# A state-space convolution beside a gated feed-forward on one core: plain loads turned by PE, paired exponentials, phases by constants, and a new order

## The chip, the cores and the metric

One core of a Trainium2 chip runs the kernel. The metric is the device time of one execution in microseconds (us), lower is better. The engines are PE (matmuls), PEld (its weight loads), DVE (VectorE), ACT (ScalarE), POOL (GpSimd) and SP, which issues most DMAs.

## The reference

Two branches get the same input u (2048 x 640, bf16) and are mixed by a gate per row.

```python
g = sigmoid((u * gate_w).sum(-1))
# branch A: a long convolution per channel d (640), kernel K from 128 complex modes n
dt = exp(log_dt);  logdA = dt * (A_re + 1j*A_im)
K[d, l] = real(sum_n C[d,n] * exp(logdA[d,n] * l) * dt * B[d,n])      # l = 0..2047
a = causal_conv(u, K) + u * Dskip                                     # by FFT of 4096
# branch B: gated feed-forward, F = 1728
b = (gelu(u @ w_gate) * (u @ w_up)) @ w_down
out = g * a + (1 - g) * b
```

## The kernel before, in words

The channels are cut into five parts of 128. The modes n lie on the partitions while the table for K is made. l is split as l = a + b: 21 coarse values a (A_OF, line 23) and 32 fine values, multiples of 8 (b_of, line 33). For each group of parts (0 and 1, 2 and 3, 4 alone: GROUPS, line 313) the kernel makes

- the magnitudes exp(a x value) on ACT (exps, line 289; 32 fine values in eB, 21 coarse ones in eA, one instruction each, over 256 elements a partition for two parts and 128 for one). a32 is A_re x dt, b32 is A_im x dt in parts of a turn (scaled_a, line 283);
- the phases on DVE as integers (trig, line 322): for coarse values one scalar_tensor_tensor a value (L337), for the 17 fine values one broadcast product a chunk with a column of values xv (L340), a quarter turn added (L344), then two sines on ACT (L352), whose low 16 bits wrap by themselves;
- the products of the two (ktable, line 447: L462 to L479), which PE then contracts over n (contract, line 483) to K, written to DRAM and gathered back (gather, line 502).

The convolution is done with matrices of sines and cosines (dft_matrix, line 387, ten in DFT and one that becomes ME) as matmuls: u folded and transformed (u_fold, u_forward), K transformed (k_forward), spectra multiplied on DVE (products, line 665), transformed back (inverse) and unfolded to the output with the feed-forward's part and Dskip's added by PE (unfold, line 724). The feed-forward's first half is ffn_up (line 511): 56 units of ten matmuls of 512 columns, from u transposed (xT) and weights, each copied out of PSUM by ACT or DVE and stored to DRAM (GUd); its second half is glu_load, glu (gelu on ACT, product on DVE) and down.

Everything is ordered by the list ORDER (line 37), whose steps a loop at the end walks. A step is a letter, one or two numbers and, where there is a copy out of PSUM, the engine for it: A for ACT, D for DVE, M for half and half. s starts the sine reciprocal, a is scaled_a, e exponentials, v the products of B and C (phase_and_size), r0 to r2 square root, half angle and angle, t trig, q ktable, c contract, w gather, u ffn_up, m a matrix, F U K P I J Z the convolution's stages, l G D the feed-forward's second half, h the gate, L the load of w_down, and ! releases memory for the next stage. The helpers table() and first() hold the order of ACT's table functions and of DVE's first steps; for the rest, the trace shows that an engine's order is not always the list's (L340 of a later step runs in the middle of v).

The beginning stands ahead of the list, in lines 205 to 308. SP loads log_dt, then A, C, B (re and im) with six transposing DMAs (loadT, line 195) and u with ten more (load_x, line 200), so that xT is in place by DMA alone. POOL issues the first weights and small vectors and zeroes a part of GUd (line 234). DVE fills small columns (c2, ncol, msk, lines 250 to 278) and makes flip, flipn and diag, from POOL's iotas.

Of the kernel before, what the change touches and what calls it, by code (L numbers as in the profile page):

```python
# [9 lines left out]
ALU = mybir.AluOpType  # L10
ACT = mybir.ActivationFunctionType
FP32 = mybir.dt.float32
# [25 lines left out]
s a e03 v e00 e13 e01 uA e04 r0 uD e02 e10 e15 uD uD uD r1 t05 uD uD uD r2 uD uD e12 uD uD e14 uD uD uA !0 uA e11 uA  # L38
uA uA e05 uA t04 q04 t06 t01 t02 q06 uD t07 uA q07 uA uA uA uA q05 t00 q00 uA m uA uA uA q02 t03 q01 t14 q03 c00A !1 m
uD c02A c01A uA t16 c10A w0 c11D uA c12A t10 uA uA m uA uA uA uA t15 uA t17 uD uD m q10 q15 uD uA m uD t11 e21 uA uD  # L40
e25 e23 e20 e24 uD q14 e22 t12 uA q16 uA q12 t13 m q17 w1 uA m uA q13 uA q11 uD c20A c21A m c22A m c30A c32A uA m t22
c31A uA w3 m !2 t20 F0P U00A q20 t21 U02A U03A t23 K00D l00 K01A U01A G00 h q22 w2 q21 q23 L c40A !3 c41A F1A U10A
D00A c42A U12A l01 U11A K10A U13A F2A U20A P00 K11A l10 G01 P01 U23A K20A D01A P10 U22A F3A D03D P02 I00A w4 P03 G10
D02A P11 U21A U30A P12 U31A K21A J10A U32D U33D D10A D11A l11 G11 P20 F4A P13 l20 D13D I01A J11A D12A G20 Z00A Z01M
K30A U40A K40A I11A l21 P21 U42A D20A K31A P22 P23 D21A l30 J20A J21A G21 K41A D23D G30 D22A P30 l31 P31 Z02A U43A
U41A D30A P32 D31A P40 P33 J22A G31 I30D P41 J23A D32A D33A J33A P42 Z11A Z03A J32A J40A J41A P43 Z12A Z10A Z20D J43D
Z13M J42A Z21M Z23A Z22D
# [4 lines left out]
def kernel(  # L52
# [49 lines left out]
    last_first = [None]  # L102

    def first(inst):
# [6 lines left out]
        return inst  # L111

# [23 lines left out]
    NMAT = 10  # L136
    DFT = cp.tile([128, NMAT, 2, 512], BF16, name="DFT")
    ME = cp.tile([128, 3, 2, 512], BF16, name="ME")
    diag = cp.tile([128, KT_, 128], BF16, name="diag")
# [5 lines left out]
    nc.vector.memset(KTt[:, 5], 0.0)  # L145
# [30 lines left out]
    NT = 3  # L176
    wg_v = B_w_gate.rearrange("(k p) f -> p k f", p=128)
# [22 lines left out]
    def load_x(hf):  # L200
        for kt in range(KT_):
            nc.sync.dma_start_transpose(out=xT[:, kt, 1024 * hf:1024 * (hf + 1)],  # L202
                                        in_=u2[1024 * hf:1024 * (hf + 1), kt * 128:(kt + 1) * 128])

    fr_i = pw.tile([128, 2, 2, 128], I32, name="fr_i")
# [6 lines left out]
    first(nc.vector.tensor_copy(out=tcol[:], in_=tcol_i[:]))  # L212
    fr = pd.tile([128, 512], FP32, name="fr")
    first(nc.vector.tensor_scalar(out=fr[:], in0=fr_i[:].rearrange("p a b q -> p (a b q)"), scalar1=TURN / 4096.0,
                                  scalar2=None, op0=ALU.mult))

    ldt = pw.tile([N, D], BF16, name="ldt")
# [8 lines left out]
    load_x(0)  # L226
    load_x(1)
    dskc = pw.tile([128, KT_], BF16, name="dskc")
    nc.gpsimd.dma_start(out=dskc[:], in_=A_Dskip.rearrange("(k p) -> p k", p=128))
    nc.gpsimd.dma_start(out=gwc[:], in_=gate_w.rearrange("(k p) -> p k", p=128))  # L230
    zero = pw.tile([128, 2, 512], BF16, name="zero")
    nc.gpsimd.memset(zero[:], 0.0)
    for c in range(4):
        nc.gpsimd.dma_start(out=GUd[c][FR:128, NFULL], in_=zero[FR:128])
# [4 lines left out]
    nc.vector.tensor_copy(out=xv[:], in_=xv_i[:])  # L239

# [5 lines left out]
    par_i = pw.tile([128, 1], I32, name="par_i")  # L246
    nc.gpsimd.iota(par_i[:], pattern=[[0, 1]], base=0, channel_multiplier=1)
    hi_i = pw.tile([128, 1], I32, name="hi_i")
    b_i = pw.tile([128, 1], I32, name="b_i")
    nc.vector.tensor_scalar(out=hi_i[:], in0=par_i[:], scalar1=16, scalar2=None, op0=ALU.bitwise_and)  # L250
    nc.vector.tensor_scalar(out=hi_i[:], in0=hi_i[:], scalar1=0, scalar2=15, op0=ALU.is_gt, op1=ALU.mult)
    nc.vector.tensor_scalar(out=b_i[:], in0=par_i[:], scalar1=31, scalar2=None, op0=ALU.bitwise_and)
    tt(out=b_i[:], in0=b_i[:], in1=hi_i[:], op=ALU.bitwise_xor)
    nc.vector.tensor_scalar(out=par_i[:], in0=b_i[:], scalar1=1, scalar2=None, op0=ALU.bitwise_and)
    b16 = pw.tile([128, 1], FP32, name="b16")
    nc.vector.tensor_scalar(out=b16[:], in0=b_i[:], scalar1=16.0, scalar2=None, op0=ALU.mult)
    ncol = pd.tile([128, 5], FP32, name="ncol")
    c2 = pd.tile([128, 7], FP32, name="c2")
    nc.vector.tensor_scalar(out=c2[:, 0:5], in0=c2_i[:], scalar1=b16[:], scalar2=None, op0=ALU.add)
    nc.vector.tensor_copy(out=c2[:, 5:6], in_=c2[:, 4:5])  # L260
    for q, vals in ((0, (3, 1, 3, 1)), (1, (5, 3, 5, 3))):
        for g in range(4):
            nc.vector.memset(ncol[32 * g:32 * g + 32, q:q + 1], float(vals[g]))
    nc.vector.tensor_scalar(out=ncol[:, 2:3], in0=par_i[:], scalar1=-2.0, scalar2=9.0, op0=ALU.mult, op1=ALU.add)
    nc.vector.tensor_copy(out=ncol[0:64, 3:4], in_=ncol[0:64, 2:3])
    nc.vector.memset(ncol[64:128, 3:4], 0.0)
    nc.vector.memset(ncol[:, 4:5], 0.0)
    nc.vector.memset(c2[:, 6:7], 0.0)
    msk = pd.tile([128, 3], FP32, name="msk")
    nc.vector.memset(msk[:], 0.0)  # L270
    for x in range(3):
        nc.vector.memset(msk[32 * x:32 * x + 1, x:x + 1], 1.0)

    for mq, nq, r, c2v, nv in ((2, 0, 0, 256 + 257, 2), (3, 1, 0, 512 + 514, 3), (4, 2, 32, 1024 + 1028, 5),
                               (5, 3, 32, 1022 + 1028, 7), (5, 3, 64, 1532 + 1535, 4),
                               (6, 4, 0, 2 * 511, 1), (6, 4, 32, 1022 + 1023, 2), (6, 4, 64, 2044 + 2047, 4)):
        nc.vector.memset(c2[r:r + 1, mq:mq + 1], float(c2v))
        nc.vector.memset(ncol[r:r + 1, nq:nq + 1], float(nv))
    dtb = pw.tile([N, D], BF16, name="dtb")
    a32 = pp.tile([N, D], FP32, name="a32")  # L280
    b32 = pp.tile([N, D], FP32, name="b32")

    def scaled_a():
        table(nc.scalar.activation(out=dtb[:], in_=ldt[:], func=ACT.Exp))
        first(tt(out=a32[:], in0=AreT[:], in1=dtb[:], op=ALU.mult))  # L285
        first(nc.vector.scalar_tensor_tensor(out=b32[:], in0=AimT[:], scalar=TURN / (2.0 * math.pi), in1=dtb[:],
                                             op0=ALU.mult, op1=ALU.mult))

    def exps(p0, np_, x0, x1):

        src = a32[:, p0 * DP:(p0 + np_) * DP]
        dA, dB = tabs[p0 // 2]
        for x in range(x0, min(x1, NB_ + NA)):
            if x < NB_:
                table(nc.scalar.activation(out=dB[:, 0:np_, :, x, :],  # L295
                                           in_=src.rearrange("n (p g d) -> n p g d", p=np_, d=4),
                                           func=ACT.Exp, scale=float(8 * b_of(x))))
            else:
                table(nc.scalar.activation(out=dA[:, 0:np_, x - NB_, :], in_=src.rearrange("n (p d) -> n p d", p=np_),
                                           func=ACT.Exp, scale=float(A_OF[x - NB_])))  # L300

    make_identity(nc, ident[:])
    fl_i = pw.tile([128, 128], I32, name="fl_i")
    nc.gpsimd.iota(fl_i[:], pattern=[[1, 128]], base=-127, channel_multiplier=1)
    nc.vector.tensor_scalar(out=flip[:], in0=fl_i[:], scalar1=0.0, scalar2=None, op0=ALU.is_equal)
    nc.vector.tensor_scalar(out=flipn[:], in0=flip[:], scalar1=-1.0, scalar2=None, op0=ALU.mult)
    tt(out=diag[:], in0=ident[:, None, :].to_broadcast([128, KT_, 128]),
       in1=dskc[:, :, None].to_broadcast([128, KT_, 128]), op=ALU.mult)

    CW = 12  # L310
    CH2 = ((0, 6), (6, 11), (11, 16), (16, NA), (NA, NA + 5), (NA + 5, NA + 9), (NA + 9, NA + 13), (NA + 13, NA + NK))
    CH1 = ((0, 11), (11, NA), (NA, NA + 9), (NA + 9, NA + NK))
# [9 lines left out]
    def trig(g, ci):  # L322
# [12 lines left out]
        if x1 <= NA:  # L335
            for x in range(n):
                nc.vector.scalar_tensor_tensor(out=ph[:, x, :], in0=b32[:, dsl], scalar=float(A_OF[x0 + x] + MID),  # L337
                                               in1=phi[:, dsl], op0=ALU.mult, op1=ALU.add)
        else:
# [105 lines left out]
    past = []  # L445

    def ktable(g, ci):
        if g not in kqt:
            n = len(GROUPS[g])
            kqt[g] = (pools["kq"].tile([N, n, NA, DP], BF16, name="Q"), pools["kq"].tile([N, n, GP, NB_, 4], BF16, name="sB"))  # L450
        Q, sB = kqt[g]
# [18 lines left out]
        kn = min(k1, 16)  # L470
# [253 lines left out]
    def unfold(z, c, eng):  # L724
# [11 lines left out]
        for h, perm in enumerate(((ident, ident), (flip, flipn))):  # L736
# [4 lines left out]
            for i, k in enumerate(ko):  # L741
                for x, part in enumerate(ZG[z]):
                    nc.tensor.matmul(pZ[:, h, W * i + DP * x:W * i + DP * (x + 1)], lhsT=xt_tile(part, c, k),
                                     rhs=diag[:, part, :], start=False, stop=False)
# [10 lines left out]
    def turn_over(x):  # L755

        if x == 0:
            ictx.__exit__(None, None, None)
# [5 lines left out]
        elif x == 2:  # L764
# [6 lines left out]
            pools.update(ub=es, pm=es, spec=es)  # L771
            pools["Wd"] = wp.tile([128, NFT, D], BF16, name="Wd")
# [17 lines left out]
    for step in ORDER.split():  # L790
# [4 lines left out]
        past.append(step)  # L795
        if kind in "qt":
# [93 lines left out]
```

## Time and profile before

| what | us |
|---|---|
| median of 3 runs (338.11 to 339.29) | 338.71 |
| the profiled execution, its own time | 336.79 |
| its span | 335.0 |
| busy: PE, DVE, ACT, POOL | 288.1, 307.9, 259.5, 11.1 |
| first full run of PE's matmuls | from 22.24 |
| a32 made on DVE (L285) | at 10.16 |
| first product of spectra (L676) | at 188.2 |
| last join of them (L685) | ends 321.8 |

A row of a group reads: line, engine, operation, output<-input with shapes, count | busy us, mean ns of one | idle time before, and what ended it. A row of a timeline begins with start and duration. In a chain of waits each row is a piece of the chain that ended last: start, length, what. Busy shares in 40 slices are in tenths.

### The profile page before, as it was taken

The numbers are of one execution on the slowest core, as the hardware profiler recorded it, in microseconds if no ns is written. First come the engines' busy times: TensorE is split into PE (matmuls) and PEld (weight loads), VectorE is DVE, ScalarE is ACT, GpSimd is POOL, SyncE is SP. The second block draws the span as 40 slices with busy tenths as digits, with TensorE's granted clock in tenths as the row PEclk, the third lists the DMA queues.
The fourth block names the chain that finished last, engine by engine and source line by source line (L and its number), as shares of the span: only waits on it lengthen the run. The fifth ranks groups of instructions, "written<-read, shape, count | busy, mean of one in ns | idle before, by whom it ended". The sixth has DMA issues, their size and how long they took to land.

```text
span 335.0 us, 6177 instructions
## 1 busy us (share of the span) xinstructions
PE 288.1 (86%) x2380; PEld 176.6 (53%) x2380; DVE 307.9 (92%) x443; ACT 259.5 (77%) x414; POOL 11.1 (3%) x41
## 2 busy tenths in 40 slices
PE   0059799999999999997377996999999999999994
PEld 0014344444465444445226755685766778677773
DVE  7685999999999999989999998899999997999962
ACT  4668999997998999998799657867576575852653
POOL 8400000000000000000000000000000000000000
PEclk9999999999999999999559997999999999999999
DMA  8998565646637876624699467555446433260133
GB/s 118 217 194 212 165 203 175 225 150 203 188 125 187 197 222 203 180 100 102 121 306 259 114 170 135 150 154 156 125 115 165 119 112 112 80 173 2 49 93 80
DMA packets 106588, 51.54 MB, mean 154 GB/s; under 512 B 50400, under 2 KB 99616, under 8 KB 106560
## 3 DMA queue, kind: packets, MB, share of 16 engines
q1 hardware_dynamic: 106112, 49.98, 56.7%
q0 software_dynamic: 448, 1.18, 1.8%
q8 instruction: 18, 0.29, 0.4%
q14 instruction: 10, 0.08, 0.1%
HBM read 29.39 MB, written 18.16 MB: 142 GB/s over the span
## 4 chain that ended last, share of the span: by engine, by line
DVE 40%; PE 35%; ACT 8%; issue 6%; SPq 5%; DMA 5%; DVEq 0%; ACTq 0%
PE gu L660 11%; PE gu L522 9%; DVE ph L337 4%; DVE GU L121 4%; PE cv L718 3%; DVE Tp L676 3%; SPq L197 3%; DVE Mb L681 3%; PE cv L603 2%; DVE eB L479 2%; PE cv L585 2%; DVE ph L344 2%; PE cv L739 2%; SPq L202 2%; ACT GU L117 2%
## 5 line engine op out<-in xcount | busy, mean ns | idle before, releaser
L522 PE MATMUL gu<-xT,Wg 128*128 128x512 bf16 x280 | 72.5, 387 | 24.8 <-DMA xT<-in_A_u_dram 19.9
L660 PE MATMUL gu<-Wd,HT 128*128 128x320 bf16 x448 | 66.4, 299 | 0.0
L522 PE MATMUL gu<-xT,Wu 128*128 128x512 bf16 x260 | 66.1, 385 | 0.0
L522 PEld LDWEIGHTS <-Wg 128*128 128x128 bf16 x280 | 27.3, 98 | 59.3 <-issue 21.4
L660 PEld LDWEIGHTS <-HT 128*128 128x128 bf16 x448 | 43.3, 98 | 18.4
L352 ACT ACTIVATE T<-ph 128x1280 bf16<-128x1280 int16 (+4 forms) x40 | 48.0, 1223 | 3.5 <-DVE ph L337 2.6
L522 PEld LDWEIGHTS <-Wu 128*128 128x128 bf16 x260 | 25.7, 99 | 33.3 <-issue 3.9
L117 ACT CAST GU<-gu 128x1024 bf16<-128x1024 f32 (+1 forms) x34 | 32.8, 969 | 6.0 <-PE gu L522 6.0
L676 DVE TENSOR_TENSOR Tp<-Uf,Kf 128x6144 bf16<-128x6144 bf16 (+2 forms) x15 | 34.3, 2288 | 0.0
L647 ACT ACTIVATE HT<-HT 128x1792 bf16<-128x1792 bf16 x16 | 26.7, 1696 | 9.7 <-DMA HT<-GUd 9.6
L121 DVE CAST GU<-gu 128x1024 bf16<-128x1024 f32 (+1 forms) x22 | 26.4, 1200 | 4.9 <-PE gu L522 4.8
L295 ACT ACTIVATE eB<-a 128x256 bf16<-128x256 f32 (+1 forms) x96 | 27.1, 373 | 4.2 <-DVE a L285 4.2
L603 PE MATMUL cv<-KTt,DFT 128*128 128x128 bf16 x280 | 24.9, 221 | 5.7 <-ACT Kf L119 2.8
L681 DVE TENSOR_TENSOR Mb<-Mb,Tp 128x4096 bf16<-128x4096 bf16 (+1 forms) x15 | 29.0, 1935 | 0.3
L119 ACT ACTIVATE ob<-gu,rat 128x640 bf16<-128x640 f32 x13 | 10.2, 793 | 21.8 <-PE gu L660 19.6
L585 PE MATMUL cv<-pm,DFT 128*128 128x512 bf16 x80 | 22.4, 407 | 3.3 <-ACT pm L566 1.5
L603 PEld LDWEIGHTS <-DFT 128*128 128x128 bf16 x280 | 21.3, 99 | 3.1 <-issue 1.9
L119 ACT ACTIVATE Kf<-cv 128x512 bf16<-128x512 f32 x34 | 18.0, 598 | 2.9 <-PE cv L603 2.9
L337 DVE SCALAR_TENSOR_TENSOR ph<-b,phi 128x256 int32<-128x256 f32 (+1 forms) x63 | 20.1, 387 | 0.0
L648 DVE TENSOR_TENSOR HT<-HT,Ut 128x1792 bf16<-128x1792 bf16 x16 | 17.3, 1089 | 2.5 <-ACT HT L647 2.5
L603 PE MATMUL cv<-KTt,ME 128*128 128x128 bf16 x120 | 19.6, 225 | 0.0
L718 PEld LDWEIGHTS <-DFT 128*128 128x128 bf16 x320 | 18.7, 98 | 1.0 <-issue 0.5
(160 smaller groups left out, 488.6 us busy)
## 6 DMA issues: line engine op xcount, KB each, us to landing
GUd<-GU SPq DMA_DIRECT2D x52, 256.0 KB, 2.4
HT<-GUd SPq DMA_DIRECT2D x16, 448.0 KB, 5.4
Ut<-GUd SPq DMA_DIRECT2D x16, 448.0 KB, 4.7
Wg<-in_B_w_gate_dram SPq DMA_DIRECT2D x11, 320.0 KB, 3.7
Wu<-in_B_w_up_dram SPq DMA_DIRECT2D x11, 320.0 KB, 4.2
fo<-in_A_u_dram SPq DMA_DIRECT2D x5, 512.0 KB, 4.8
Wd<-in_B_w_down_dram SPq DMA_DIRECT2D x1, 2080.0 KB, 9.0
out_dram<-ot SPq DMA_DIRECT2D x8, 256.0 KB, 2.4
```

What stands on the lines that cost most here:

```text
L117: nc.scalar.copy(out=dst, in_=src)
L119: nc.scalar.activation(out=dst, in_=src, func=ACT.Copy, scale=scale)
L121: nc.vector.tensor_copy(out=dst, in_=src)
L337: nc.vector.scalar_tensor_tensor(out=ph[:, x, :], in0=b32[:, dsl], scalar=float(A_OF[x0 + x] + MID), in1=phi[:, dsl], op0=ALU.mult, op1=AL ...
L352: table(nc.scalar.activation(out=dst, in_=phl, func=ACT.Sin, scale=SIN_SCALE))
L522: nc.tensor.matmul(p[:, r], lhsT=W[:, kt, f0:f0 + 128], rhs=xT[:, kt, 512 * c:512 * (c + 1)], start=(kt == 0), stop=(kt == KT_ - 1))
L585: nc.tensor.matmul(pU[:, ri], lhsT=dmat(e, ri, m), rhs=pm[:, ri, e].rearrange("p c d -> p (c d)"), start=(e == 0), stop=(e == 1))
L603: nc.tensor.matmul(pW[:, ri, 128 * m:128 * (m + 1)], lhsT=lhs, rhs=rhs, start=(first and x == 0 and m == 0), stop=(x == len(seq) - 1), ski ...
L660: nc.tensor.matmul(pD[:, h, 0:DH], lhsT=HT[:, ft, 128 * e:128 * e + 128], rhs=Wd[:, ft, DH * h:DH * (h + 1)], start=(ft == 0), stop=(ft == ...
L676: tt(out=dst.rearrange("p c h r f -> p (c h) r f"), in0=U[:, c0:c1].rearrange("p c h f -> p (c h) f")[:, :, None, :].to_broadcast([128, n, ...
L681: tt(out=M, in0=M, in1=T[:, t0:t1], op=ALU.add)
L718: nc.tensor.matmul(pY[:, c % 2, 256 * r + 128 * e:256 * r + 128 * (e + 1)], lhsT=dinv(m, r, e), rhs=pst[part][c // 2][:, c % 2, 0, r, 128 ...
```

## The change

- Line order at the start: the identity is made first on POOL. A_re and A_im are loaded plainly as [128, 5, 128] and turned by ten matmuls with the identity into PSUM; log_dt and the first weights are issued on ACT. The first half of u (1024 rows) is loaded plainly in two pieces (into buffers of T) and turned by PE, four matmuls a channel part and piece, with six copies to xT (step x: four on DVE, two on ACT). The second half still comes by five transposing DMAs, issued at the new step y.
- a32 holds a and 2a; exps makes two values, v and 2v, in one instruction where both are wanted. Values of zero are filled by POOL. e's numbers mean other values than before. e03 stands twice in the new list.
- In trig, the fine phases of groups of two parts are one product with a constant a value; the value zero is dropped, so that chunks are 4 x 4 for 5, 4, 4, 4.
- The column steps and the flips become steps i0 and i1, in a forced order on DVE. diag is made at "!2". The zeroes of GUd are written from SP at "!0".
- A new list.

```diff
 ORDER = """
-s a e03 v e00 e13 e01 uA e04 r0 uD e02 e10 e15 uD uD uD r1 t05 uD uD uD r2 uD uD e12 uD uD e14 uD uD uA !0 uA e11 uA
-uA uA e05 uA t04 q04 t06 t01 t02 q06 uD t07 uA q07 uA uA uA uA q05 t00 q00 uA m uA uA uA q02 t03 q01 t14 q03 c00A !1 m
...
+s a e03 x02D x00D x01A i1 e00 x10D e01 x11A e03 x12D e04 v i0 y uD r0 e02 uD uA e15 uA uD e10 e05 uD uD uD t05 r1 uD
+uA uD r2 uA uD e14 e11 uD e12 uD uA e13 uA t04 uA t07 !0 uA q04 uA t01 uA uA uA t06 uA t02 uA q07 q06 t00 uA m uA uA
...
+uA uD c20A c21A c22A c30A uA m c32A m t22 c31A t20 uA !2 F0P w3 m t21 l00 U00A t23 q22 U03A q20 U02A K00D K01A U01A
+G00 w2 L h q21 q23 c40A !3 c41A F1A c42A U10A U12A l01 U11A K10D D00A F2A U13A U20D P00 K11A P01 G01 K20A l10 U23A
+D01A D03D F3A l11 P02 U22A G10 P03 P10 I00A K21A D02A U21A P11 U30A D10A U31A U33D P20 P12 l20 D11A U32D G11 P13 l21
+F4A D13D w4 G20 I10A I01A D12D Z01M K30A Z00A D20A U40A P21 I11A K40A P22 l30 D21A U42A I20A G21 K31M P23 D23D K41D
+l31 G30 D22A P30 Z02A P31 P32 U41A D30A U43A P33 G31 D31A I30D P40 J33D D32A I21A P41 P42 D33A Z11A P43 Z03A J41A J32A
+J40A Z12A Z10A Z20D J43D J42A Z22M Z21M Z23D Z13D
 """
...
-    ldt = pw.tile([N, D], BF16, name="ldt")
-    nc.sync.dma_start(out=ldt[:], in_=A_log_dt.partition_broadcast(N))
-    wt[0] = load_w(0, nc.gpsimd.dma_start)
-    AreT = loadT(A_A_re, "AreT")
-    AimT = loadT(A_A_im, "AimT")
+    nc.scalar.dma_start(out=ldt[:], in_=A_log_dt.partition_broadcast(N))
+    nc.sync.dma_start(out=Are_n[:], in_=A_A_re.rearrange("(k p) n -> p k n", p=128))
+    nc.sync.dma_start(out=Aim_n[:], in_=A_A_im.rearrange("(k p) n -> p k n", p=128))
+    nc.sync.dma_start(out=xn[0], in_=u2[0:512].rearrange("(t p) d -> p t d", p=128))
+    wt[0] = load_w(0, nc.scalar.dma_start)
+    nc.sync.dma_start(out=xn[1], in_=u2[512:1024].rearrange("(t p) d -> p t d", p=128))
     CreT = loadT(A_C_re, "CreT")
...
-    load_x(0)
-    load_x(1)
...
+    def turn_x(q, i, eng):
+        pX = psC.tile([128, 2, 512], FP32, name="cv")
+        ks = range(2 * i, min(2 * i + 2, KT_))
+        for e, kt in enumerate(ks):
+            for t in range(4):
+                nc.tensor.matmul(pX[:, e, 128 * t:128 * (t + 1)], lhsT=xn[q][:, t, 128 * kt:128 * (kt + 1)],
+                                 rhs=ident[:], start=True, stop=True)
+        dst, src = xT[:, ks[0]:ks[-1] + 1, 512 * q:512 * (q + 1)], pX[:, 0:len(ks)]
+        if eng == "A":
+            table(nc.scalar.copy(out=dst, in_=src))
+        else:
+            first(nc.vector.tensor_copy(out=dst, in_=src))
...
-        first(tt(out=a32[:], in0=AreT[:], in1=dtb[:], op=ALU.mult))
...
+        for t in (Are_n, Aim_n):
+            p = psF.tile([128, 2, 512], FP32, name="gu")
+            pA.append(p[:].rearrange("p e x -> p (e x)")[:, 0:D])
+            for k in range(KT_):
+                nc.tensor.matmul(pA[-1][:, 128 * k:128 * (k + 1)], lhsT=t[:, k], rhs=ident[:], start=True, stop=True)
+        first(tt(out=a32[:, 0], in0=pA[0], in1=dtb[:], op=ALU.mult))
+        first(nc.vector.tensor_scalar(out=a32[:, 1], in0=a32[:, 0], scalar1=2.0, scalar2=None, op0=ALU.mult))
...
+    def chain2(values):
+        out, left = [], [v for v in values if v]
+        while left:
+            v = min(left)
+            pair = (v, 2 * v) if 2 * v in left else (v,)
...
+        elif np_ == 2:
+            for x in range(n):
+                nc.vector.tensor_scalar(out=ph[:, x, :], in0=b32[:, dsl], scalar1=float(8 * (NK - 1 - x0 - x + NA)),
+                                        scalar2=None, op0=ALU.mult)
         else:
             tt(out=ph, in0=b32[:, None, dsl].to_broadcast([N, n, W]),
                in1=xv[:, x0 - NA:x1 - NA, None].to_broadcast([N, n, W]), op=ALU.mult)
...
         if x == 0:
+            for c in range(4):
+                nc.sync.dma_start(out=GUd[c][FR:128, NFULL], in_=zero[FR:128])
```

Counted over the whole list, the copies out of PSUM that change their engine are: one unit of ffn_up and one of contract from DVE to ACT; from ACT to DVE K10 (six copies of 512), K41 (two), half of K31 (one), U20, D12, J33 and some output tiles at the end.

More of the change, by code (lines that the diff above doesn't have):

```diff
@@ L111, in first, with chain @@
         return inst
+    def chain(inst):
+        return first(inst)
     def copy(eng, dst, src, scale=None):
@@ L136 @@
     NMAT = 10
+    SLOT = {b_of(x): x for x in range(NB_)}
+    assert SLOT[16] == NB_ - 1
     DFT = cp.tile([128, NMAT, 2, 512], BF16, name="DFT")
     ME = cp.tile([128, 3, 2, 512], BF16, name="ME")
-    diag = cp.tile([128, KT_, 128], BF16, name="diag")
     ident = cp.tile([128, 128], BF16, name="ident")
@@ L249 @@
     b_i = pw.tile([128, 1], I32, name="b_i")
[L250 to L254, printed above, removed]
@@ L279, with flips @@
+    def flips():
+        chain(nc.vector.memset(KTt[:, 5], 0.0))
+        chain(nc.vector.tensor_scalar(out=flip[:], in0=fl_i[:], scalar1=0.0, scalar2=None, op0=ALU.is_equal))
+        chain(nc.vector.tensor_scalar(out=flipn[:], in0=flip[:], scalar1=-1.0, scalar2=None, op0=ALU.mult))
     dtb = pw.tile([N, D], BF16, name="dtb")
-    a32 = pp.tile([N, D], FP32, name="a32")
+    a32 = pp.tile([N, 2, D], FP32, name="a32")
     b32 = pp.tile([N, D], FP32, name="b32")
@@ L302 @@
[L302 to L308, printed above, removed]
@@ new lines, in scaled_a @@
+        first(tt(out=a32[:, 0], in0=pA[0], in1=dtb[:], op=ALU.mult))
+        first(nc.vector.tensor_scalar(out=a32[:, 1], in0=a32[:, 0], scalar1=2.0, scalar2=None, op0=ALU.mult))
+        first(nc.vector.scalar_tensor_tensor(out=b32[:], in0=pA[1], scalar=TURN / (2.0 * math.pi), in1=dtb[:],
+                                             op0=ALU.mult, op1=ALU.mult))
+        first(nc.vector.tensor_copy(out=xv[:], in_=xv_i[:]))
+    def chain2(values):
[3 more added lines that the diff above has]
+            pair = (v, 2 * v) if 2 * v in left else (v,)
+            for x in pair:
+                left.remove(x)
+            out.append(pair)
+        return out
@@ L795 @@
         past.append(step)
+        if kind == "u" and ups[0][0] < 2:
+            after(*(f"x{ups[0][0]}{i}" for i in range(3)))
+        elif kind == "u":
+            after("y")
+        elif kind == "m":
+            after("s", *(("i0",) if len(mats) <= NMAT - 3 else ()))
+        elif kind == "!" and x == 0:
+            after("i0", "i1", "r2")
         if kind in "qt":
@@ L819 @@
             dft_first()
+        elif kind == "x":
+            turn_x(x, y, eng)
+        elif kind == "y":
+            load_x(1)
+        elif kind == "i":
+            (columns, flips)[x]()
         elif kind == "a":
```

137 lines of the change are left out of this document (81 added, 56 removed).

## Prediction

> **What bounds the kernel now.** I read the page's busy shares and slices first, then busy times by stretch, then the chain of work that ended last, then VectorE's own timeline and the groups by shape.
>
> ```profile
> PE 288.1 (86%) x2380; PEld 176.6 (53%) x2380; DVE 307.9 (92%) x443; ACT 259.5 (77%) x414; POOL 11.1 (3%) x41
> ...
> PE   0059799999999999997377996999999999999994
> ...
> DVE  7685999999999999989999998899999997999962
> ACT  4668999997998999998799657867576575852653
> ```
>
> VectorE (DVE) is nearly full from slice 5 to 39, PE has its holes at the start and in slices 19 to 21. The stretches (columns: length, then PE, PEld, DVE, ACT, POOL busy) put numbers to it:
>
> ```profile
> 0.00:10.00 10.00, 0.00 (x0) 0.10 (x1) 6.00 (x29) 3.93 (x4) 8.38 (x35) 1.00 0.85 126
> 10.00:20.00 10.00, 1.59 (x3) 0.31 (x3) 8.94 (x30) 8.99 (x30) 2.74 (x7) 1.00 1.21 218
> 20.00:30.00 10.00, 8.51 (x26) 3.05 (x25) 5.21 (x7) 7.16 (x19) 0.00 (x0) 1.00 0.96 194
> 30.00:188.00 158.00, 142.01 (x977) 71.68 (x975) 154.73 (x265) 147.25 (x236) 0.00 (x0) 0.96 0.63 181
> 188.00:322.00 134.00, 127.71 (x1283) 94.69 (x1280) 128.54 (x103) 87.39 (x116) 0.00 (x0) 0.99 0.46 121
> 322.00:335.00 13.00, 8.31 (x103) 6.77 (x100) 4.49 (x13) 4.76 (x13) 0.00 (x0) 0.99 0.40 101
> ```
>
> DVE's 27.1 us of idle lie like this: 9.85 before 30 us, 3.3 from 30 to 188 (188.2 is the first product, L676), 5.5 from 188 to 322, 8.5 in the tail. So in the middle the time is DVE's work, and the start is another matter. The chain there, and DVE's rows beside it:
>
> ```profile
> 6.41 3.53 SPq L197
> ...
> 17.77 4.43 DMA xT<-in_A_u_dram
> 22.24 6.28 PE gu L522 x16
> 28.54 1.23 DVE GU L121
> ```
> ```profile
> 10.03 0.15 DVE L250 TENSOR_SCALAR hi_i<-par_i 128x1 int32<-128x1 int32 x1 [1.83 <-POOL par_i L247]
> 10.16 0.82 DVE L285 TENSOR_TENSOR a<-AreT,dtb 128x640 f32<-128x640 bf16 x1
> ...
> 28.54 1.23 DVE L121 CAST GU<-gu 128x1024 bf16<-128x1024 f32 x1 [4.76 <-PE gu L522]
> ```
>
> The start hangs on transposing loads in one SP queue: u's land so that PE's first full run of matmuls begins at 22.24, and DVE stands 4.76 us for it. And a, from which all exponentials are made, comes at 10.16, queued behind a column instruction that waits for POOL; ACT stands 4.2 us for a.
>
> **The change, part by part.** All durations are start to start on a busy engine, unless said. The sum is made on DVE.
>
> Start, work added. Turning adds four DVE copies out of PSUM: two of 128x1024 at 1.14 (the casts of L121 follow each other at that) and two of 128x512 at 0.61: 3.5 us. 2a is one 128x640 operation with a constant: 0.41 (L368 to L369). a and b read PSUM instead of SBUF; between 0 and 0.2 us more, I take 0. On ACT two copies, 2.0. On PE 50 matmuls of 128 columns: 128/512 of the 0.43 that the first matmuls take is 0.11, 5 us in all, in a stretch where PE is idle. The three loads issued on ACT cost 0.3 to 0.6 each by SP's rows; ACT waits 2.1 us for fr there anyway. If that cover went, under 2 us would fall on ACT's first table load.
>
> Start, idle. In the new order DVE goes straight from the reciprocal (ends 8.2) to a, 2a, b, xv (0.74 + 0.41 + 0.77 + 0.1): 10.2. Plain loads of 160 KB land in 3.4 to 3.5 us (ldt, KTt) and of 512 KB in 4.8 (fo), so A is in PSUM by then and u's first quarter about then. x02 and x00 end at 12.0, flips (0.33 + 0.15 + 0.15) at 12.6, x10 and x12, which each wait for a PSUM buffer and some 1 us of PE, near 15.5. The B/C product chain (nine of 0.74, two of 0.41: 7.5) runs to 23, the columns (some 3.5: 27 fills in 1.6 us, a dozen small steps of 0.14) to 26.5. Their work adds up to 22, so idle is 4.5 where it was 9.85. PE can begin ffn_up at about 15. Bounds: if B and C, now behind 1.3 MB of u in SP's queue, land at 18 instead of 15, idle is 7.5. I take 5.3, i.e. a gain of 4.5. The new wait is that of the first u copies: on DVE they stand behind v and the columns if emission order holds (L340 between two parts of v shows that it does not always), and PE, with two PSUM buffers, waits behind them until 23 to 26.5; it still has two units done then where it had one.
>
> Phases as products with constants. 32 instructions of 256 elements replace eight broadcast products (six of 1024 at 1.14, two of 1280 at 1.41: 9.7).
>
> ```profile
> 66.61 1.77 DVE L337 SCALAR_TENSOR_TENSOR ph<-b,phi 128x256 int32<-128x256 f32 x5
> ...
> 71.16 1.23 DVE L340 TENSOR_TENSOR ph<-b,xv 128x1024 int32<-128x1024 f32 x1
> ```
> ```profile
> L383 DVE TENSOR_SCALAR phi<-vi 128x640 f32<-128x640 f32 x1 | 0.5, 485 | 0.0
> ```
>
> No row is this instruction. L337 does 256 in 0.336 with two tensors. L383 does 640 in 0.40 to the next start against 0.74 for a product of two tensors: one tensor and a constant run twice as fast. L412, 256 with a column, follows at 0.26. Half of 0.27 plus the 0.07 of L337 is 0.205: 6.6 in all, a gain of 3.1. Bounds: 0.26 gains 1.3, 0.336 loses 1.1. I take 0.205, by L383, the only row with a plain constant. [...]
>
> One step fewer of 17 in the phases: L344, L477, L479 lose 0.13 each and L476 0.07 in two groups, half that and 0.13 of L340 in the third: -1.3.
>
> List, up to the first product: one u copy and one Kraw copy go from DVE to ACT, -1.14 and -1.0. diag (0.74) only moves from the start to "!2"; t20 and one matrix change places across "!2". Sum before the first product: 3.5 + 0.4 - 3.1 - 1.3 - 2.1 = -2.6, and -4.5 of idle: **-7.1**.
>
> List, after it: ACT gives DVE copies of Kf (K10: six, K41: two, K31: one, 0.61 each: 5.5), Uf (U20, 1.14), ob (D12, 0.8), pr (J33, 0.6): +8.0, and output tiles in the tail, 1.4, which lie in its 8.5 us of idle. What hides part of the 8.0: DVE waits there 2.5 for gelu (L648 for L647) and 1.4 for pm, both ACT's, and ACT loses about 8 us of copies; I let those 3.9 go: **+4.1**. Bounds: all 8.0 hidden (PE is the bound there, 6.3 idle of 134) or none.
>
> ACT: exponentials of 256 follow at 0.318 (nine in 2.86); 512 cost 0.318 + 256 x 0.0009 (sin of 1280 less sin of 1024) = 0.55, so a pair saves 0.09. With 15 pairs and two values fewer a group, 5.7 in three groups; shorter sines 1.1; less 2.0 for turning and 1.0 because e03 stands twice in the list (three exponentials made again): 3.8 saved. It is cover, not path: DVE is fuller. If pairs cost as two, 4 us of it go and ACT is even with before. The zero writes of GUd move from POOL to SP at "!0", four issues of 0.4 in a queue that mostly waits: nothing; what could wait for them is the first table in the reused space, 4 us from issue to landing.
>
> Sum: -7.1 + 4.1 = **-3.0** on the profiled execution (span 335.0, time 336.79). That execution is 1.9 under the median of 338.71; the same difference gives **335.7**.
>
> **Rivals.**
> 1. All of the start is kept: PE bounds the second half, the 8 us of copies fall into DVE's gaps. For it: PE is 95% busy from 188 to 322, and waits 2.8 us for ACT's Kf once, just where K10 goes to DVE. Against: DVE is 96% busy there. -7.1: 331.6.
> 2. Slower: DVE bounds the second half. None of the copies is hidden, and the start gains 2 of idle only: -2.6 - 2.0 + 8.0 = +3.4, 342.1. It decides if the products (L676 to L685) end later against their start than now: 188.2 to 321.8, 133.6 us. Against: 3.9 us of DVE's waits there are for ACT.
> 3. The start comes late: u's and B/C's loads share the queues, x11 on ACT stands behind e01, the first u copy behind the columns, so that idle falls by 1.5 only: no change, 338.7.
> 4. The small constants cost a full instruction each, as L412's 0.35 when nothing overlaps: 11 us for 9.7 instead of 6.6, loses 4.5 of the sum: +1.5, 340.2. [...]
>
> **How the numbers follow.** Forecast 0.36, rivals in order 0.24, 0.24, 0.10, 0.06. A measurement here tells about 0.3% (1.0 us) from no change. Faster: 0.30 of the forecast's (its own range is -5 to -1), 0.24, 0.03 of the third, 0.01 of the fourth: 0.58. Same: 0.05 + 0.02 of the second + 0.05 + 0.02 = 0.14. Slower: the rest, 0.28. The range runs from beyond rival 1 (329) to rival 2 (342.5).
>
> **What would show it.** Right: a before 9 us; ffn_up's matmuls from about 15; DVE idle before 30 near 5; 32 constant products of 256 about 0.2 apart; first product near 181; products lasting some 138 us. DVE busy in total about 315 (307.9 - 2.6 + 8.0 + 1.4). Wrong: DVE standing for B/C or for turned tiles after 12, PE standing for the first u copy beyond 27, ACT idle unchanged beside a DVE that is full from 188 on, or the order on the engines differing from the list.

## The result, and the profile after

The changed kernel takes 339.99 us (median of 19 runs, 339.26 to 342.68), the kernel before 337.33 over 19 runs: a ratio of 1.0084, 95% interval 1.0063 to 1.0106. It is slower by some 2.7 us, where 3.0 faster was forecast. The profiled execution has a span of 337.8 (before 335.0).

Busy times, and DVE's slices, of the changed kernel's page:

```profile
PE 289.1 (86%) x2401; PEld 181.0 (54%) x2430; DVE 315.6 (93%) x486; ACT 248.0 (73%) x348; POOL 9.1 (3%) x44
...
DVE  5696899999997999899899999999999999999984
```

DVE's total is the forecast's 315. Its idle is not. The stretches (length, then PE, PEld, DVE, ACT, POOL busy, the granted clock, DMA):

```profile
0.00:10.00 10.00, 1.43 (x10) 0.90 (x10) 6.02 (x6) 4.96 (x7) 8.03 (x39) 1.00 0.81 203
10.00:20.00 10.00, 7.34 (x51) 5.28 (x53) 7.46 (x16) 5.59 (x10) 0.00 (x0) 1.00 1.27 154
20.00:30.00 10.00, 7.76 (x36) 3.21 (x35) 9.80 (x19) 6.96 (x16) 0.00 (x0) 1.00 1.02 248
30.00:189.60 159.60, 134.59 (x920) 67.52 (x933) 150.65 (x320) 147.23 (x207) 1.10 (x5) 0.96 0.61 175
189.60:326.00 136.40, 130.87 (x1300) 98.28 (x1313) 135.76 (x111) 81.07 (x104) 0.00 (x0) 0.98 0.44 119
326.00:337.80 11.80, 7.13 (x89) 5.83 (x88) 5.89 (x18) 2.16 (x6) 0.00 (x0) 1.00 0.46 113
```

DVE's idle before 30 us fell from 9.85 to 6.7, but between 30 and the first product it rose from 3.3 to 8.95. The first product is at 189.63 (before 188.22), the products last 136.4 (133.6), the tail 11.7 (13.2). So the first half lost 1.4 where 7.1 of gain were forecast, and the second lost 1.3 instead of 4.1.

Where the idle after 30 comes from is read on SP's own queue (start, length of the issue, what):

```profile
15.43 7.49 SPq L207 DMA_TRANSPOSE xT<-in_A_u_dram  x5
22.97 0.58 SPq L192 DMA_DIRECT2D Wg<-in_B_w_gate_dram  x1
...
24.24 2.60 SPq L823 DMA_DIRECT2D GUd<-zero  x4
26.93 1.65 SPq L590 DMA_DIRECT2D GUd<-GU  x2
```

and, a little later, on ACT and on DVE (idle before in brackets, with what ended it):

```profile
31.68 1.01 ACT L121 CAST GU<-gu 128x1024 bf16<-128x1024 f32 x1 [4.72 <-DMA GUd<-GU]
```
```profile
8.05 0.82 DVE L332 TENSOR_TENSOR a<-gu,dtb 128x640 f32<-128x640 f32 x1 [0.49 <-PE gu L331]
8.91 1.02 DVE L333 TENSOR_SCALAR a<-a 128x640 f32<-128x640 f32 x1
...
32.32 1.23 DVE L125 CAST GU<-gu 128x1024 bf16<-128x1024 f32 x1 [2.49 <-DMA GUd<-GU]
...
43.81 4.14 DVE L442 RECIPROCAL vr<-vr 128x640 f32<-128x640 f32 x1
```

PE's first run of five matmuls of ffn_up now begins at 18.50 (before 22.62), but the five transposing loads of u's second half (step y) hold SP for 7.5 us; the second weights are issued only at 22.97, and the zero writes of GUd, listed at "!0", have been drawn ahead of the first GU store. The stores come late, ACT and DVE stand for them, and the half-angle reciprocal starts at 43.81 (before 37.07). In absolute time SP's queue is no later than before, where the second weights were issued at 26.21 and the first store at 27.61; but ffn_up, which starts earlier, runs into it. The chain that ended last (start, length, what) runs through the same places: from y's transposes to the landing of the second weights, and then to that of the stores:

```profile
23.61 6.07 DMA Wu<-in_B_w_up_dram
30.22 4.69 DMA GUd<-GU
```

### The profile page after: what moved, and what is told of

Read it like the earlier page. It is cut to its first block, busy times and chain, and to the rows that moved or that the text cites. A ratio compares the mean times of both kernels' runs of the same rounds, so it can differ in the third digit from the quotient of the medians.

```text
span 337.8 us, 6237 instructions
## 1 busy us (share of the span) xinstructions
PE 289.1 (86%) x2401; PEld 181.0 (54%) x2430; DVE 315.6 (93%) x486; ACT 248.0 (73%) x348; POOL 9.1 (3%) x44
## 4 chain that ended last, share of the span: by engine, by line
DVE 44%; PE 25%; ACT 8%; SPq 7%; issue 7%; DMA 7%; DVEq 0%; ACTq 0%
PE gu L724 9%; PE gu L586 6%; DVE Tp L740 4%; ACT T L416 4%; SPq L202 3%; DVE Mb L745 3%; DVE GU L125 3%; DVE HT L712 3%; PE cv L782 3%; DVE ph L397 3%; DVE ph L408 2%; SPq L207 2%; PE cv L667 2%; DMA Wu<-in_B_w_up_dram 2%; ACT Kraw L121 2%
## 5 line engine op out<-in xcount | busy, mean ns | idle before, releaser
L586 PE MATMUL gu<-xT,Wg 128*128 128x512 bf16 x265 | 70.5, 385 | 10.5 <-ACT GU L121 7.2
L416 ACT ACTIVATE T<-ph 128x1024 bf16<-128x1024 int16 (+3 forms) x40 | 46.9, 1195 | 5.6 <-DVE ph L397 3.6
L121 ACT CAST GU<-gu 128x1024 bf16<-128x1024 f32 (+1 forms) x35 | 33.7, 969 | 5.4 <-DMA GUd<-GU 4.7
L125 DVE CAST GU<-gu 128x1024 bf16<-128x1024 f32 (+1 forms) x21 | 25.0, 1190 | 2.6 <-DMA GUd<-GU 2.5
L369 ACT ACTIVATE eB<-a 128x256 bf16<-128x256 f32 (+2 forms) x66 | 24.2, 450 | 2.7 <-DVE a L332 2.7
L649 PE MATMUL cv<-pm,DFT 128*128 128x512 bf16 x72 | 20.1, 378 | 5.8 <-DVE pm L638 2.3
L123 ACT ACTIVATE ob<-gu,rat 128x640 bf16<-128x640 f32 x12 | 9.5, 794 | 18.6 <-PE gu L724 18.5
L559 PE MATMUL cv<-eA,eB 128*128 128x84 bf16 x160 | 15.1, 211 | 7.4 <-ACT Kraw L121 4.5
L121 ACT CAST Uf<-cv 128x1024 bf16<-128x1024 f32 x17 | 17.0, 1017 | 5.5 <-DVE Tp L740 4.7
L667 PE MATMUL cv<-KTt,ME 128*128 128x128 bf16 x120 | 18.8, 219 | 0.0
```

Of the source, the lines that this page charges most:

```text
L121: nc.scalar.copy(out=dst, in_=src)
L125: nc.vector.tensor_copy(out=dst, in_=src)
L369: table(nc.scalar.activation(out=dst, in_=src, func=ACT.Exp, scale=float(scale)))
L416: table(nc.scalar.activation(out=dst, in_=phl, func=ACT.Sin, scale=SIN_SCALE))
L586: nc.tensor.matmul(p[:, r], lhsT=W[:, kt, f0:f0 + 128], rhs=xT[:, kt, 512 * c:512 * (c + 1)], start=(kt == 0), stop=(kt == KT_ - 1))
L667: nc.tensor.matmul(pW[:, ri, 128 * m:128 * (m + 1)], lhsT=lhs, rhs=rhs, start=(first and x == 0 and m == 0), stop=(x == len(seq) - 1), ski ...
```

## The experiments

Every ratio is to the kernel before on the same chip, with its 95% interval; stage times are of one profiled execution each, which can lie 2 us beside the median (e6: 334.32 and 336.11), so that small differences rest on the ratios. The theories: **Q**, SP's queue at the start costs the time; **C**, the copies given to DVE in the second half do; **L**, the new list does; **B**, the bytes loaded at the start do; **R**, the order that falls out when the instructions are scheduled at compile time does, which any edit reshuffles; and against R in the later runs **W**, the work or the engines' load itself.

**Zero writes late (e1), and y late too (e2).** e1 orders the four zero writes on SP behind the tenth GU store; e2 also puts y's five transposes behind the stores 5, 7, 9, 11, 13.

```diff
-                nc.sync.dma_start(out=GUd[c][FR:128, NFULL], in_=zero[FR:128])
+                behind(nc.sync.dma_start(out=GUd[c][FR:128, NFULL], in_=zero[FR:128]), 9)
...
-            nc.sync.dma_start_transpose(out=xT[:, kt, 1024 * hf:1024 * (hf + 1)],
+            behind(nc.sync.dma_start_transpose(out=xT[:, kt, 1024 * hf:1024 * (hf + 1)],
```

> The changed kernel with one edit: the four zero writes of GUd, which the trace of the changed kernel shows on SP at 24.24 to 26.84 ahead of the first store of GU (26.93), are put behind the tenth store. Theory Q (SP's queue at the start eats the start's gain): the first two stores go out about 2.6 us earlier, the waits of ACT (4.7) and DVE (2.5) for GUd<-GU near 32 us fall by about that, and the ratio to the kernel before goes from 1.008 to 1.002, if nothing further on takes it back. Theory L (the new list's first half holds DVE up elsewhere, whatever the start): those waits fall, the first product of spectra still begins near 189.7 and the ratio stays at 1.007 to 1.009. Theory C (the copies given to DVE in the second half): ratio stays at 1.008.

> As the run before, and the five transposing loads of u's second half, on SP from 15.43 to 22.9 ahead of the second weights (issued at 22.97), are spread behind the 5th, 7th, 9th, 11th and 13th store. Theory Q: the second weights are issued near 16, PE no longer stands for them (1.4 and 0.8 us) nor for the copies (1.8), DVE's idle from 30 to 40 goes from 3.7 to under 1, and the ratio comes to 0.99 to 0.997. Theory L: the first 40 us gain 4 to 5 us of idle and the first product still begins after 187; ratio 1.000 to 1.006. Theory C: ratio as without the edit, 1.005 to 1.009.

e1: 339.54, ratio 1.0073 (1.0043 to 1.0103). e2: 337.16, 1.0009 (0.9984 to 1.0033). SP's queue in e2, and DVE's stretch from 30 us to the first product (columns as above):

```profile
15.49 0.58 SPq L199 DMA_DIRECT2D Wg<-in_B_w_gate_dram  x1
...
21.94 2.21 SPq L597 DMA_DIRECT2D GUd<-GU  x2
```
```profile
30.00:186.08 156.08, 133.70 (x913) 67.24 (x926) 150.41 (x322) 144.63 (x205) 1.06 (x5) 0.94 0.67 186
```

The second weights go 7.5 us earlier, DVE's wait for the stores is gone, its idle in that stretch falls from 8.95 to 5.67, the reciprocal starts at 40.50, the first product at 186.1. Q's mechanism holds: freeing the queue regains as much as the whole loss. By the ratios the transposes are most of it (e1 keeps 1.0073); by the first product they are 1.9 of 3.5 us (e1: 188.0). Q's ranges (1.002 for e1, 0.990 to 0.997 for e2) were missed: e2 is only level with the kernel before, and the forecast gain is still missing.

**Copies back (e3) and the old list (e4).** e3 gives K10, K41, K31, U20, D12, J33 back to ACT; e4 runs the new code in the old order, with the steps x, i, y set in at the start.

```diff
-G00 w2 L h q21 q23 c40A !3 c41A F1A c42A U10A U12A l01 U11A K10D D00A F2A U13A U20D P00 K11A P01 G01 K20A l10 U23A
+G00 w2 L h q21 q23 c40A !3 c41A F1A c42A U10A U12A l01 U11A K10A D00A F2A U13A U20A P00 K11A P01 G01 K20A l10 U23A
...
```

> The changed kernel, with the copies out of PSUM of the second half that went from ACT to DVE given back to ACT (K10, K41, K31, U20, D12, J33: 8.0 us of DVE's work; the output tiles stay). Theory C: DVE is 99.6% busy from 189.7 to 322, so 8 us less work there ends it 4 to 8 us sooner; ratio 0.985 to 0.997. Theories Q and L: the second half of the changed kernel is only 1.3 us longer than before with 8.7 us more work on DVE, so DVE's added copies mostly took the place of waits; giving them back gains 0 to 2 us, ratio 1.003 to 1.009.

> The changed kernel's code under the list of before, with the new steps set in at the start (x02 x00 x01 i1 x10 x11 x12 ahead of v, then i0 and y). Theory L: the new list's order is at fault, and the code's savings (4.4 us of DVE's work for phases, 5.7 of ACT's for pairs) show: ratio 0.985 to 0.997. Theory Q: the same queue of transposes and zero writes stands ahead of the first stores, so the start loses as much; ratio 1.000 to 1.010. Theory C: the old list has the old letters in the second half, so ratio 0.985 to 0.997 too, and the run before tells L and C apart.

345.88, 1.0259 (1.0217 to 1.0301), and 345.73, 1.0259 (1.0226 to 1.0293). Both are far above what C and L expected. C falls: in e3, without the copies, DVE's idle during the products grows from 0.6 to 11.2. The order was not held in e3, but beside the twelve copies only 15 of DVE's instructions and 4 of ACT's change places in its trace. e3's waits (who waited for whom: us, times, longest):

```profile
DVE Ma L740 <- PE cv L782: 5.1, 2, 3.5
DVE HT L712 <- ACT HT L711: 3.4, 4, 1.5
```

L finds no support: in e4 the first product comes at 190.2, no sooner than in the changed kernel, and the products, with the old letters, take 139.0 with 10.4 of idle, much as in e3. What e4's own instruction order does to its time was not tried.

**ACT's issues (e6).** e2 with the first weights issued on SP instead of ACT (and POOL's iota for fr ahead of the identity). DVE's and PE's instructions keep their order.

```diff
-    wt[0] = load_w(0, nc.scalar.dma_start)
+    wt[0] = load_w(0, nc.sync.dma_start)
```

> As e2, with the first weights issued on SP behind u's first quarter instead of on ACT, and POOL's fr_i ahead of the identity. ACT's first table load then starts near 1.2 instead of 2.25 and the sine reciprocal on DVE near 3.3 instead of 4.21. If the wait of DVE for the sine is on the path: a 0.9 us sooner and ratio 0.997 to 1.000. Theory B (the loads' bytes set the start: DMA engines are full from 3 to 33 us): a waits for A_re (landed at 7.2 in the changed kernel) whatever ACT does, the turned tiles wait as long, and the ratio stays at 1.000 to 1.002.

336.11, 0.9991 (0.9962 to 1.0019). In the changed kernel ACT's first table load began at 2.25, behind three issues; in e6:

```profile
1.20 1.28 ACT L505 ACT_TABLE_LOAD   x1 [1.20 <-PEq L964]
```

DVE's reciprocal of the sines starts 1.06 earlier, a (6.61) 1.4 earlier than in the changed kernel, and the first product is at 183.7. The ratio's interval overlaps e2's (1.0009), so a gain in time is likely, not shown.

**Fills (e5, e10).** Both put the 23 constant column fills ahead of fr on DVE, e5 on e2, e10 on e6. In e5's trace 79 of DVE's 486 instructions, the fills among them, and 28 of ACT's have changed places beside e2. In e10 every engine is held in e6's order but for the fills: each instruction is tied behind the one that preceded it there, by dependencies of the class NoSync.

```diff
+        for g in range(4):
+            first(nc.vector.memset(ncol[32 * g:32 * g + 32, q:q + 1], float(vals[g])))
...
+def hold(tc):
+    by_name = {i.name: i for i in tc.nc.all_instructions()}
...
+                    tc.add_manual_dep(inst, last,
```

> The kernel of the run that spread the transposes (e2), with 23 of the 31 small constant fills of the columns put back ahead of fr on DVE, where it stands 1.6 us for POOL. Theory Q (what stands on the path in the first 40 us reaches the end): the fills took some 2.0 us between 36.9 and 40.8 in the changed kernel and cost about 0.5 here where they outlast the wait for fr, so first product 1 to 1.5 us sooner, ratio to before 0.996 to 0.999. Theory R (the instruction order that falls out of the list decides, small gains are lost in it): ratio anywhere from 0.998 to 1.006.

> e6 with the 23 constant fills ahead of the first cast on DVE, as in e5, but all other instructions of every engine held in e6's order. Theory R: e5's loss of 2.8% was the order that the edit brought about, so it goes: the fills leave the path (about 1.5 us between 30 and 40) and put at most 1 us on the start, ratio 0.994 to 1.000 against before, half-angle reciprocal at 36.5 to 37.5 where e6 has 38.0. Theory W (the fills at the start delay fr and all behind it): slower than e6, ratio 1.01 to 1.03.

e5: 345.14, 1.0282 (1.0237 to 1.0327). e10: 335.11, 0.9968 (0.9942 to 0.9994), the reciprocal at 36.52, the first product at 182.7. The same edit costs 2.7% beside e2 (1.0009) where the order is free, and nothing beside e6 (0.9991) where it is held; whether it gains there is not shown, as the intervals of e6 and e10 overlap. The two bases differ by e6's edit, which is far too small for the difference, so R holds here. In e5 DVE waits for the zero writes, and 4.2 us for PE and ACT before the products Q (1.4 in e2):

```profile
61.44 0.69 DVE L550 TENSOR_TENSOR sB<-T,eB 128x1024 bf16<-128x1024 bf16 x1 [3.25 <-DMA GUd<-zero]
```

**Constants alone (e7, e9).** The kernel before with the phases by constants; in e9 every engine held in the order of the kernel before.

```diff
+        elif np_ == 2:
+            for x in range(n):
+                nc.vector.tensor_scalar(out=ph[:, x, :], in0=b32[:, dsl], scalar1=float(8 * (NK - 1 - x0 - x + NA)),
```

> The kernel before with one part of the change alone: the fine phases of groups of two parts as products with constants (34 of 256 elements for eight broadcast products). Rows of the changed kernel: x4 in 0.81 to 1.0 start to start against 1.14 for 1024. DVE's work falls by 2.5 to 3 us; since DVE is 98% busy from 30 to 188 the first theory (DVE's work is the time there) gives ratio 0.991 to 0.995. Theory R: the same list gives another order, and the ratio lies anywhere between 0.993 and 1.008.

> The kernel before with the phases as products with constants, as in e7, but with every engine's instructions held in the order of the kernel before (each of eight broadcast products replaced in its place by its 4 or 5 small ones, 34 in all). Theory R (e7 gained nothing because the rebuilt order took it back): 34 products 0.20 to 0.25 apart are 7 to 8.5 us where eight products took 9.7, so DVE's path is 1.2 to 2.7 us shorter and the ratio is 0.992 to 0.997, the first product near 186. Theory W (the saved DVE work was not on the path, another engine sets the pace in the middle): ratio 1.000 to 1.003 as in e7, with DVE's idle between 30 and 188 us grown by about 2.

336.66, 1.0022 (0.9993 to 1.0052), and 336.47, 1.0014 (0.9978 to 1.005). R falls here: in e9 the order is the same (in e7, too, only 9 other instructions of DVE change places), the 34 products take 6.89 us from start to next start for the 9.60 of eight broadcast ones, and still the first product comes only 1.1 us earlier (187.1) and no change of the time can be told. The stretch from 100 to 150, first of e9, then of the kernel before (columns as above):

```profile
100.00:150.00 50.00, 48.69 (x274) 22.78 (x273) 46.53 (x87) 48.12 (x92) 0.00 (x0) 1.00 0.62 180
```
```profile
100.00:150.00 50.00, 49.23 (x272) 22.96 (x269) 48.02 (x87) 48.50 (x92) 0.00 (x0) 1.00 0.65 185
```

DVE got 1.5 us less to do from 100 to 150 and stood for them: PE and ACT are 96 to 98% busy there, and DVE's waits for PE grow from 0.3 to 1.0, those for ACT from 1.5 to 2.3. In the middle three engines bound the time together.

**Pairs alone (e8, e12, e13).** The kernel before with paired exponentials and 2a (diag moved to "!2" for room). In e12 DVE, PE and SP are held in the order of the kernel before, in e13 ACT's sines and copies too. Between e12 and e13 some fifteen instructions of ACT change places, and nothing else.

```diff
-    a32 = pp.tile([N, D], FP32, name="a32")
+    a32 = pp.tile([N, 2, D], FP32, name="a32")
...
+            pair = (v, 2 * v) if 2 * v in left else (v,)
```

> The kernel before with the paired exponentials alone (2a made on DVE, zeroes filled by POOL, diag made at the step !2 as the room needs it). ACT's work falls by about 5.7 us, DVE's grows by 0.4 to 0.9. If ACT is only cover: ratio 0.998 to 1.004. If ACT bounds the stretch from 30 to 150 as much as DVE (121 of 127 us busy): ratio 0.988 to 0.997. Theory R: above 1.004, by another order.

> The kernel before with the paired exponentials, 2a and diag moved to !2, as in e8, but DVE, PE and SP held in the order of the kernel before (2a right behind a, diag behind the instruction that it is emitted after); ACT's order is free. Theory R: e8's 3.1% was the order, and is gone: DVE has 0.5 to 1 us more work, ACT 3 to 5 us less, ratio 0.996 to 1.006. Theory W (pairs themselves cost: longer single instructions on ACT, a later first table): ratio above 1.015, with DVE standing for exponentials' tables by 5 us or more.

> e12 (the kernel before with paired exponentials; DVE, PE, SP in its order) with ACT's other instructions, sines and copies, held in the order of the kernel before as well; only the exponentials' places between them are free. Against e12 nothing else differs: on ACT some ten instructions change places, above all two sines of 1408 that e12 has behind the pm copies, which wait 4.5 us for PE. Theory R (order): e12's 2.9% goes, ratio 0.996 to 1.006, the first product at 187 to 190 where e12 has 196.4, DVE's wait for the sines under 1 us. Theory W (pairs themselves cost): ratio stays above 1.015.

346.24, 1.0306 (1.0264 to 1.0347); 345.72, 1.0291 (1.025 to 1.0332); 337.54, 1.0048 (1.0013 to 1.0083). My expectation that holding three engines would do was wrong; the fourth decided. ACT in e12, then DVE:

```profile
170.54 1.01 ACT L585 CAST pm<-cv 128x1024 bf16<-128x1024 f32 x1 [4.49 <-PE cv L584]
...
177.09 6.13 ACT L371 ACTIVATE T<-ph 128x1408 bf16<-128x1408 int16 x5
```
```profile
178.50 0.89 DVE L482 TENSOR_TENSOR Q<-T,eA 128x1408 bf16<-128x1408 bf16 x1 [5.45 <-ACT T L371]
```

and ACT in e13:

```profile
168.41 1.38 ACT L371 ACTIVATE T<-ph 128x1408 bf16<-128x1408 int16 x1 [2.38 <-DVE ph L356]
170.00 1.38 ACT L371 ACTIVATE T<-ph 128x1408 bf16<-128x1408 int16 x1 [0.22 <-DVE ph L363]
171.29 1.91 ACT L585 CAST pm<-cv 128x1024 bf16<-128x1024 f32 x2
```

Two sines that stand behind two waiting copies in one queue, instead of ahead of them, make DVE stand 5.45 of the 8.0 us between the two profiled executions. (The copies wait because PE itself stands 5.08 us there for the load fo, 4.21 in e13.) Pairs by themselves gain nothing here either (1.0048, and the interval lies above 1): they relieve ACT, but DVE has 1.7 us more work up to the first product. Of that, 2a is 0.4, and three short steps at 13 us, where POOL has its fills of the value zero, last 0.86 to 1.07 for 0.14 to 0.23 in the kernel before and add about 0.8 (last section); what of it reaches the end is not shown.

**u by transposing loads (e11, e14).** e11 is e6 with the first half of u by five DMA transposes, ahead of C and B on SP, instead of plain loads and PE's turning; the rest held in e6's order. e14 adds e10's fills.

```diff
-    nc.sync.dma_start(out=xn[0], in_=u2[0:512].rearrange("(t p) d -> p t d", p=128))
-    nc.sync.dma_start(out=xn[1], in_=u2[512:1024].rearrange("(t p) d -> p t d", p=128))
+    load_x(0)
     CreT = loadT(A_C_re, "CreT")
```

> e6 with the first half of u by five DMA transposes instead of two plain loads, 40 matmuls on PE and six copies; all else in e6's order, the transposes on SP where the plain load of the second quarter stood. The prediction's step (turning pays: ffn_up starts early, DVE's idle at the start falls by 4.5 for 3.5 of copies): without it ffn_up begins about 3 to 5 us later, first product 1 to 3 us later than e6, ratio 1.002 to 1.010. Rival (the copies cost more than the early start gives): 3.5 us of DVE work go and B and C come later, first product earlier by 1 to 3 us, ratio 0.990 to 0.997.

> e11 (first half of u by DMA transposes) with the 23 constant fills ahead of fr on DVE as in e10, all other instructions in e11's order. The fills take some 1.5 us from between 33 and 37 us and go into DVE's idle at the start (9.9 us in e11, of which 6.0 wait for B and C). Theory R: first product about 1.5 us earlier than e11's 184.7, ratio 0.991 to 0.996. Rival (PE and ACT bound the middle, as e9 suggests: DVE's gain is given back): ratio 0.996 to 0.999.

334.64, 0.9975 (0.9953 to 0.9998), and 334.45, 0.9933 (0.9898 to 0.9969). Without turning u PE's first run of five begins at 15.53 (16.63 in e6). The first product comes 1.0 later than in e6, as the prediction's step said (1 to 3), but the ratio lies below its range and is not worse than e6's. DVE waits for B and C instead:

```profile
17.27 0.82 DVE L433 TENSOR_TENSOR va<-CreT,BreT 128x640 f32<-128x640 bf16 x1 [6.02 <-DMA BreT<-in_A_B_re_dram]
```

and its idle before 30 is 9.95 again, but six copies less stand on DVE and ACT. The early start can be had by u standing ahead of C and B in SP's queue; PE's turning is not needed for it. e14's fills bring the reciprocal 1.0 earlier (38.95) and the first product not at all (184.8 for 184.7): that fits the rival's mechanism, though the ratio lies in R's range. The medians of e11 and e14 cannot be told apart. e14 is the fastest version by its ratio, faster than both kernels; its interval overlaps those of e10, e11 and e15.

**y late in the kernel before (e15).** Only u's second half moves behind the stores there; the rest is held.

```diff
-    load_x(1)
...
+            if hf == 1:
+                behind(inst, 4 + 2 * kt)
```

> The kernel before with one edit: the five transposing loads of u's second half go behind the stores 5, 7, 9, 11 and 13 on SP, as in e2, and do not stand ahead of the second weights any more; all engines otherwise in the order of the kernel before. If the queue costs the kernel before what it costs the changed one (Theory Q everywhere): second weights issued near 19 instead of 26.2, ratio 0.990 to 0.996. Rival (in the kernel before the queue hides behind the late first matmuls, DVE's wait of 4.8 us for PE at 28.5 starts with u's first half, not with the weights): ratio 0.998 to 1.003.

334.74, 0.9967 (0.9932 to 1.0001). Second weights at 18.86 instead of 26.21. PE's third run of five matmuls, in e15 and then in the kernel before:

```profile
25.50 1.24 PE L530 MATMUL gu<-xT,Wu 128*128 128x512 bf16 x5
```
```profile
26.88 1.62 PE L522 MATMUL gu<-xT,Wu 128*128 128x512 bf16 x5
```

The first product is at 186.4 (188.2). PE's first run of five already begins 1.0 earlier (21.58), because u's first half lands sooner, so the gain is not the weights' alone. In this execution the products also last 2.1 less (131.5), for which the start gives no reason. The interval touches 1, and the ratio lies between the two expectations: that the queue cost time before the change as well is likely and not certain.

## Why the prediction was wrong, step by step

The step that failed is **start, idle: -4.5**, with the idle behind it, from 30 us to the first product, taken as unchanged. Measured to the first product, DVE's idle rose by 2.5. The step's first part came out in part: a at 8.05 (forecast before 9), the second turned copy done at 14.7 (12.0), ffn_up's first single matmul at 15.84 (about 15) and its first run of five at 18.50, idle before 30 lower by 3.1. What I left out is SP's queue behind it. I priced the zero writes "in a queue that mostly waits: nothing" and y not at all, although it is a step that is moved and holds SP 7.5 us. e2 gives their price: 0.75% of 337, 2.5 us. The landing estimates were wrong as well: u's pieces of 640 KB took 10.1 and 12.6 us and A_re's 160 KB 6.4, for my 4.8 (512 KB) and 3.4. All these loads are issued in the first 3.8 us; that this is the reason (theory B) was not tried. And the issues on ACT, which I let hide under ACT's wait for fr, put off its first table load by 1.05.

The first product was forecast at 181.1 and came at 189.6. Of these 8.5 us about 1.5 are work, 1.4 are idle before 30, and 5.7 are idle between 30 and the first product. The queue is 3.3 of the 5.7, which e2 takes away. The other 2.4 stay in e2, where DVE's waits are for ACT and PE (the longest 1.1, 0.8, 0.8 and 0.6); no run took them apart.

- **Work, -2.6**: measured -1.1. The constants were right: in e9, 0.203 each (0.205). One of them lasts 0.28 to 0.29 there, but four took 0.81 from start to start, so that rival 4's full length each (0.35) is not borne out. a and b, read from PSUM, lasted 0.82 each in the changed kernel (0.82 and 0.85 before). 2a took 0.94 instead of 0.41; the rest of the 1.5 was not separated.
- **The frame**: that the middle "is DVE's work" was half true. e9 took 2.7 us off DVE with the order held, and no change of the time could be told. The sum on one engine overstated what it bought: from 100 to 150 PE was 97% and ACT 96% busy beside it.
- **Second half, +4.1**: the mechanism was right, the size not. DVE's idle during the products fell by 4.6 (3.9 forecast), the products grew by 2.8, and the tail, where DVE took output copies and which I had put at nothing, was 1.5 shorter: +1.3.
- **Pairs as cover, not path**: agrees with e13, which is 0.5% slower. That e03 stands twice was not tried by itself.
- **Rivals**: the sign is rival 2's, its mechanism is not (the second half lost 1.3). Rival 3, the start comes late, is nearest, by the queue it names and at another place. That the order could differ from the list stood among the signs of error and had no price; e12 beside e13 and e5 beside e10 give it one, 2.4 and 3.1%.

Left open: how much of the 2.5 us that e2 regains is the stores' and how much the second weights'; and whether the changed kernel's own order, in the middle, hides a further loss of e12's kind.

## What to carry to other kernels

Walk each DMA queue past the change as you walk the engines: a step moved ahead of weights and stores has a price there, whatever its data are for; here y held SP for 7.5 us. Where several engines are as busy as in e9 (PE 97%, ACT 96%, DVE 93% from 100 to 150), count a saving only as far as the next of them allows. And when an edit changes the time by some per cent, first compare the engines' orders: hold the order and measure the edit again, on all engines. With ACT's order free the ratio was 1.0291 (e12), with it held 1.0048 (e13).

## What the runs showed of the hardware

Three short operations of DVE took 1.00 to 1.07 us near POOL's memsets. POOL's four memsets for the value zero run from 8.49 to 9.58 in the changed kernel, and 2a, from 8.91, took 1.02 (shown above). In e6, where POOL likewise has 39 instructions before 10 us and none from 10 to 20, 2a comes earlier and took 0.50, and the cast xv at 8.62 took 1.00 (0.17 in the changed kernel, at 10.60). In e13 POOL has 11 instructions from 10 to 20 for 7 in the kernel before (the four memsets are what its edit adds), and flip took 1.07 (0.23 in the kernel before). Rows of e6 and of e13:

```profile
7.47 0.50 DVE L340 TENSOR_SCALAR a<-a 128x640 f32<-128x640 f32 x1
...
8.62 1.00 DVE L343 CAST xv<-xv_i 128x17 f32<-128x17 int32 x1
```
```profile
13.05 1.07 DVE L326 TENSOR_SCALAR flip<-fl_i 128x128 bf16<-128x128 int32 x1 [0.21 <-POOL fl_i L325]
```

Beside POOL's iotas the same cast took 0.11 (8.08 in the kernel before). fr took 1.27 in the kernel before, where POOL issued DMAs from 1.53 to 5.38, and 0.50 in the changed one, beside POOL's iotas and the last step of the identity. That POOL's work makes these differences is my reading of the rows; no run varied it alone.

A transposing load's issue held SP 1.27 us for each of C and B in e11, and 1.30 to 1.94 for u's second half in the changed kernel. There it held SP 4.62, 2.78 and 2.71 us for CreT, BreT and CimT, which stand behind 1.3 MB of u; what holds them was not tried.
